# GpSimd scales the softmax weights of the first six attention tiles, and the first phase is written in a new order

## The chip, the cores and the metric

The kernel runs on one core of one Trainium2 chip. Time is device microseconds (us) of one execution; the kernel before has a median of 427.57 us over 3 runs (426.88 to 429.05). Engines: TensorE (PE; PEld is its weight load), VectorE (DVE), ScalarE (ACT), GpSimd (POOL) and SyncE (SP), which issues the DMAs.

## The reference

Three layers in a row, batch 4, sequence 576. Only the first two lie in the part that changes.

```python
# 1: windowed attention, 8 heads of 64
scores = scale * np.matmul(q, k.transpose(0, 1, 3, 2))
mask = (rel >= 0) & (rel < window)            # window = 128
scores = np.where(mask, scores + bias[None], -1000000000.0)
attn = np.exp(scores - max); attn = attn / (attn.sum(-1) + 1e-09)
x = np.matmul(attn, v)
# 2: gated MLP
h = np.maximum(x @ w_in, 0.0); u, v = halves of h
v_n = (v - mean) / sqrt(var + 1e-6)
v_s = w_spatial @ v_n (over the sequence) + b_spatial
x = (u * v_s) @ w_out
# 3: mixture of 4 attention experts, two of them gated in per token (second phase)
```

## The kernel before

**Two phases.** The first phase (up to about 246 us) does layers 1 and 2 up to the gated product, which goes to DRAM. Then follow a fold of `w_out` with the experts' weights, and the second phase, layer 3. Only the first phase changes.

**Tiles and names.** The first attention runs over 20 tiles of 128 queries (the fifth of each batch has 64), numbered 0 to 19 in the order of the list `tiles`; tile n has two groups of four heads, g = 0 and 1. The work is written out by hand as a list of steps, the string `OPENING` (then `FIRST` and `SECOND`): for each engine the order of its instructions is that of the list, and each engine works through its own queue in that order, waiting where data or a buffer is not there. `step()` (L807) turns a name into instructions:

- `rawN`, `qN`, `kN`, `vN`, `Wk.ld`: loads, on SyncE's queue. `CN.x`: turns the 64-bit words of chunk N of `w_in` into two fp32r parts `win`: abs, high, low on ScalarE; shl, or, mask, mul, rest on VectorE (L439 to L442, L263); sum, add, minus, sec on TensorE.
- `sN.g`: scores, TensorE, into one of two `psS` buffers. `lN.g.cp` (L551, L543) and `lN.g.i` (L285): masking copy and row minimum, VectorE. `eN.g.i` (L286): exponential with row sum, ScalarE. `fN.g.add`, `.rec` (L562, L563): the sum's reciprocal, VectorE. `fN.g.mul` (L566): the weights times it, VectorE.
- Tiles 0 to 5 are turned on TensorE: `tN.g` (L615), `cN.g` copies to SBUF (L617, ScalarE), `gN.g.0` and `.1` mask the two key blocks (L624, L625, GpSimd). Tiles from 6 on are "carried": `mN.g` (L565) scales the weights on GpSimd, and they are turned through DRAM (`T`, `w`, `R`).
- `aN` (L648): weights times values, TensorE. `xhN` and `xlN` (L698, L263): high and low part of x, ScalarE and VectorE. `psT` has one buffer: every `t` and every `a` of tiles 0 to 5 takes it in turn, and the next waits until `c`, or `xh` and `xl`, have read it.
- `Vb.t.n` (L712), `Ub.s.m.n` (L775), `Pb.m.s.n` (L790): three passes each of the products with `w_in` and `w_spatial`, TensorE; `r`, `bn`, `ag`, `n`, `N`, `ur`, `pm` take and normalise their results.
- `W0.ld` also issues `pads()` (L481): two memsets of `vtail` and two fills of `vt` on GpSimd (L483, L485).

What a carried and an uncarried tile differ in stands here:

```python
        if carried(b, j):
            ops["m"] = lambda: nc.gpsimd.tensor_tensor(blocks, blocks, sm.unsqueeze(1).unsqueeze(3).to_broadcast([P, 4, n, 32]), op=ALU.mult)
        ops["f.mul"] = lambda: nc.vector.tensor_tensor(p[:, :n, :], p[:, :n, :], sm.unsqueeze(2).to_broadcast([P, n, P]), op=ALU.mult)
```

Of the kernel before, what the change touches and what calls it, by code (L numbers as in the profile page):

```python
# [23 lines left out]
P = 128  # L24
# [21 lines left out]
    l2.1.0 l2.1.1 f1.0.add C2.mask l2.1.2 l2.1.3 C3.or C2.mul f1.0.rec C3.mask e1.1.0 c0.0 C1.low e1.1.3 e1.1.1 C2.high e1.1.2 a0 C2.sum C2.minus s3.1
    C2.sec C3.sum e2.1.3 e2.1.2 xh0 C4.abs C3.high f1.1.add f1.0.mul xl0 f1.1.rec C3.mul f1.1.mul e2.1.0 e2.1.1 C2.low t1.0 c1.0 C3.minus C3.sec
    C3.low t1.1 V0.0.0 V0.0.1 V0.0.2 C5.abs c1.1 g1.0.0 g1.0.1 g1.1.0 g1.1.1 l2.0.cp f2.1.add l2.0.0 l2.0.1 l2.0.2 l2.0.3 f2.1.rec C5.shl e2.0.3
    e2.0.2 e2.0.1 e2.0.0 f2.1.mul l3.1.cp t2.1 l3.1.0 f2.0.add l3.1.1 f2.0.rec l3.1.2 f2.0.mul l3.1.3 s3.0 r0.0 c2.1 t2.0 c2.0 e3.1.3 e3.1.2 s4.1
    g2.1.0 g2.1.1 g2.0.0 g2.0.1 a1 C5.or l3.0.cp l3.0.0 l4.1.cp l3.0.1 e3.1.1 e3.1.0 l3.0.2 l3.0.3 e3.0.3 xh1 e3.0.0 e3.0.1 l4.1.0 l4.1.1 C4.shl C4.or  # L50
    xl1 e3.0.2 f3.1.add f3.1.rec f3.1.mul C5.mask f3.0.add C5.mul C4.mask C4.mul f3.0.rec C5.high raw6 v3 v4 raw7 W0.ld k5 e4.1.0 e4.1.1 s4.0 q5 q6
    W1.ld W1.hi q7 s5.0 a2 xh2 W0.hi V0.1.0 V0.1.1 V0.1.2 C6.abs C7.abs C4.high xl2 f4.1.add f4.1.rec C5.rest f4.1.mul C6.shl C7.shl f3.0.mul t3.1
    C5.add C5.sec c3.1 V0.2.0 t3.0 V0.2.1 g3.1.0 g3.1.1 l4.0.cp C7.or l4.0.0 l4.0.1 c3.0 v5 v6 k10 v7 v8 C4.rest r0.1 g3.0.0 s5.1 C7.high l5.0.cp
    C7.mask C5.low t4.1 q8 V0.2.2 g3.0.1 c4.1 l5.0.0 e4.0.0 l5.0.1 l5.1.cp e4.0.1 C7.rest C4.add g4.1.0 a3 r0.2 l5.1.0 l5.1.1 e5.0.0 f4.0.add C7.mul
    g4.1.1 e5.0.1 e5.1.0 f4.0.rec C6.or e5.1.1 s6.0 v10 xh3 f4.0.mul s6.1 C6.high f5.0.add xl3 C7.add q9 V0.3.0 f5.0.rec C6.rest f5.0.mul t4.0 C6.mask
    C7.sec c4.0 C4.sec l6.0.0 C7.low C6.mul g4.0.0 t5.0 C4.low V0.3.1 l6.0.1 l6.0.2 O0.ld c5.0 l6.0.3 e6.0.0 g4.0.1 f5.1.add V0.3.2 g5.0.0 e6.0.1
    l6.1.0 f5.1.rec bn0.0 e6.0.2 g5.0.1 e6.0.3 a4 f5.1.mul r0.3 l6.1.1 l6.1.2 e6.1.0 l6.1.3 s7.1 f6.0.add bn0.1 v13 xh4 v14 e6.1.1 f6.0.rec xl4 C6.add
    m6.0 e6.1.2 U0.0.0.0 e6.1.3 bn0.2 U0.0.0.1 f6.1.add T6.0 C6.sec t5.1 C6.low s7.0 f6.1.rec l7.1.cp w6.0 m6.1 c5.1 O0.abs bn0.3 U0.0.3.0 l7.1.0
    g5.1.0 U0.0.1.0 l7.1.1 e7.1.0 l7.1.2 g5.1.1 l7.1.3 e7.1.1 T6.1 q14 s8.0 e7.1.2 O1.ld ag0.0 e7.1.3 ag0.1 ag0.2 w6.1 ag0.3 W0.lo n0.2.ln U0.0.0.2
    n0.2.ex f7.1.add a5 n0.2.r0 W1.lo ur0.0.0 f7.1.rec n0.2.r1 O0.shl W4.ld m7.1 U0.0.1.1 l7.0.cp U0.0.2.0 n0.2.r2 R6.0 U0.0.2.1 l7.0.0 l7.0.1 W2.ld  # L60
    U0.0.3.1 e7.0.0 l7.0.2 l7.0.3 e7.0.1 T7.1 U0.0.3.2 e7.0.2 U0.0.1.2 n0.2.r3 e7.0.3 O0.or R6.1 U0.0.2.2 ur0.0.3 w7.1 f7.0.add ur0.0.1 l8.0.cp s8.1
    xh5 f7.0.rec N0.2.sc ur0.0.2 m7.0 xl5 U0.1.1.0 N0.2.hi U0.1.2.0 l8.0.0 q10 W4.hi l8.0.1 l8.0.2 U0.1.1.1 T7.0 e8.0.0 U0.1.1.2 W2.hi l8.0.3 V0.4.0
    N0.0.sc w7.0 ur0.1.1 N0.1.sc e8.0.1 N0.0.hi U0.1.3.0 W4.lo N0.1.hi U0.1.3.1 l8.1.cp e8.0.2 R7.1 V0.4.1 W2.lo e8.0.3 W3.ld l8.1.0 a6 l8.1.1 W5.ld
    e8.1.0 l8.1.2 l8.1.3 e8.1.1 f8.0.add N0.2.lo U0.1.2.1 xh6 f8.0.rec N0.0.lo e8.1.2 U0.1.2.2 m8.0 e8.1.3 R7.0 xl6 V0.4.2 ur0.1.2 f8.1.add s9.1
    N0.1.lo g7.1.0 r0.4 f8.1.rec T8.0 V1.0.0 W5.hi m8.1 l9.1.cp w8.0 V1.0.1 bn0.4 W3.hi g7.1.1 l9.1.0 V1.0.2 l9.1.1 e9.1.0 l9.1.2 g7.0.0 l9.1.3 e9.1.1
    ag0.4 W5.lo U0.1.3.2 n0.4.ln g7.0.1 r1.0 U0.1.0.0 ur0.1.3 T8.1 U0.1.0.1 n0.4.ex e9.1.2 n0.4.r0 W3.lo e9.1.3 s9.0 w8.1 n0.4.r1 f9.1.add a7 bn1.0
    l9.0.cp n0.4.r2 R8.0 f9.1.rec l9.0.0 xc7 U0.1.0.2 m9.1 l9.0.1 q11 l9.0.2 e9.0.0 l9.0.3 k15 s14.1 xs7 ur0.1.0 v11 e9.0.1 s10.1 n0.4.r3 T9.1 xh7
    e9.0.2 N0.3.sc w9.1 V1.1.0 e9.0.3 N0.4.sc N0.3.hi xl7 V1.1.1 N0.4.hi N0.3.lo g8.0.0 P0.0.1.0 l14.1.cp R8.1 f9.0.add U1.0.0.0 l14.1.0 g8.0.1
    l14.1.1 V1.1.2 f9.0.rec e14.1.0 ag1.0 N0.4.lo m9.0 e14.1.1 U1.0.0.1 r1.1 P0.0.1.1 f14.1.add P0.0.0.0 P0.0.1.2 bn1.1 P0.0.0.1 T9.0 R9.1 P0.0.0.2
    l10.1.0 f14.1.rec w9.0 ag1.1 l10.1.1 e10.1.0 U1.0.0.2 m14.1 l10.1.2 e10.1.1 l10.1.3 pm0.0.0 s14.0 g8.1.0 e10.1.2 T14.1 ur1.0.0 s10.0 pm0.0.1  # L70
    e10.1.3 g8.1.1 q13 O0.mask P0.1.1.0 q12 f10.1.add w14.1 P0.1.0.0 O0.mul P0.1.1.1 f10.1.rec g9.1.0 O0.add U1.0.1.0 P0.1.0.1 m10.1 O2.ld P0.1.0.2
    l14.0.cp O0.hi R9.0 l14.0.0 gs0.0 l14.0.1 P0.1.1.2 e14.0.0 pm0.1.0 g9.1.1 O0.sh e14.0.1 T10.1 U1.0.1.1 O1.abs pm0.1.1 U1.0.1.2 w10.1 f14.0.add
    O0.lo a8 ur1.0.1 l10.0.0 f14.0.rec O1.shl e10.0.0 m14.0 l10.0.1 l10.0.2 s11.1 e10.0.1 l10.0.3 O0.sl O1.or xc8 R14.1 g9.0.0 s11.0 T14.0 v12 e10.0.2
    xs8 e10.0.3 gs0.1 P0.2.0.0 g9.0.1 w14.0 O1.mask xh8 P0.3.0.0 P0.2.0.1 xl8 P0.2.0.2 l11.1.cp R10.1 P0.3.0.1 f10.0.add O1.mul q15 P0.3.1.0 pm0.2.0
    g14.1.0 O3.ld P0.3.0.2 l11.1.0 l11.1.1 e11.1.0 l11.1.2 g14.1.1 l11.1.3 V1.2.0 e11.1.1 f10.0.rec O1.add m10.0 e11.1.2 e11.1.3 pm0.3.0 P0.3.1.1
    O1.hi l11.0.cp V1.2.1 O2.abs O1.sh T10.0 P0.2.1.0 l11.0.0 l11.0.1 w10.0 P0.3.1.2 e11.0.0 l11.0.2 l11.0.3 e11.0.1 f11.1.add O1.lo V1.2.2 e11.0.2
    pm0.3.1 e11.0.3 f11.1.rec O2.shl s13.1 r1.2 O1.sl m11.1 f11.0.add gs0.3 s12.1 bn1.2 a9 f11.0.rec T11.1 m11.0 ag1.2 O2.or xc9 R14.0 P0.2.1.1 R10.0
    n1.2.ln P0.2.1.2 n1.2.ex w11.1 xs9 U1.0.3.0 pm0.2.1 xh9 U1.0.3.1 l13.1.cp U1.0.3.2 xl9 v15 V1.3.0 ur1.0.3 l13.1.0 v16 l13.1.1 e13.1.0 l13.1.2
    l13.1.3 gs0.2 V1.3.1 e13.1.1 T11.0 g14.0.0 e13.1.2 n1.2.r0 e13.1.3 s13.0 w11.0 O2.mask g14.0.1 n1.2.r1 V1.3.2 l12.1.cp n1.2.r2 f13.1.add l12.1.0
    U1.1.1.0 q16 r1.3 l12.1.1 l12.1.2 U1.0.2.0 l12.1.3 e12.1.0 n1.2.r3 bn1.3 U1.1.0.0 e12.1.1 e12.1.2 N1.0.sc U1.1.1.1 e12.1.3 ag1.3 N1.2.sc a10  # L80
    n1.3.ln N1.0.hi N1.1.sc n1.3.ex f13.1.rec N1.2.hi f12.1.add l13.0.cp m13.1 U1.1.0.1 N1.1.hi n1.3.r0 U1.1.1.2 l13.0.0 U1.0.2.1 ur1.1.1 n1.3.r1
    l13.0.1 e13.0.0 l13.0.2 U1.1.0.2 l13.0.3 e13.0.1 n1.3.r2 N1.0.lo U1.0.2.2 ur1.1.0 U1.1.3.0 e13.0.2 n1.3.r3 N1.2.lo ur1.0.2 U1.1.3.1 xh10 N1.3.sc
    U1.1.2.0 e13.0.3 N1.1.lo N1.3.hi U1.1.2.1 xl10 U1.1.3.2 N1.3.lo a14 ur1.1.3 f13.0.add T13.1 s12.0 xc14 R11.1 f13.0.rec R11.0 xs14 s15.1 m13.0
    f12.1.rec w13.1 O2.mul xh14 U1.1.2.2 m12.1 P1.0.0.0 ur1.1.2 T13.0 P1.0.0.1 q19 xl14 P1.0.0.2 w13.0 P1.1.0.0 T12.1 P1.1.0.1 g11.1.0 pm1.0.0
    P1.1.0.2 O2.add g11.0.0 w12.1 P1.0.1.0 O2.hi pm1.1.0 P1.1.1.0 l12.0.cp g11.1.1 O3.abs P1.0.1.1 O2.lo g11.0.1 R13.1 P1.0.1.2 O2.sh l12.0.0 l12.0.1
# [1284 lines left out]
```

## Time and profile before

| | |
|---|---|
| median of 3 runs | 427.57 us (426.88 to 429.05) |
| the profiled execution | 427.63 us, its span 425.5 us |
| TensorE busy | 411.5 us (97%) |
| VectorE busy | 315.3 us (74%) |
| ScalarE busy | 243.9 us (57%) |
| GpSimd busy | 156.2 us (37%) |
| mean granted TensorE clock | 0.997 |

The profile is of one execution; its own time is 427.63 us, of which the span from the first to the last instruction is 425.5. "Busy" is the time in which an engine has an instruction under way, so neighbours that overlap count once. A matmul's end is modelled. In a row, `[1.57 <-PE pt L615]` behind an instruction says that its engine was idle 1.57 us before it and what ended that. Rows of one instruction on VectorE or ScalarE overlap the next by a little; the chain of waits counts from start to start.

### The profile page before, as it was taken

The page shows a single profiled execution, that of the slowest core. Times are in us where ns is not written, and L with a number is a line of the kernel's source. Part 1 is how long each engine was busy: PE and PEld are TensorE (multiplying, and loading weights), DVE is VectorE, ACT ScalarE, POOL GpSimd, SP SyncE. Part 2 cuts the span into 40 slices and gives each one's busy share as a digit, 9 for nine tenths or more (in the row PEclk, how much of TensorE's full clock was granted, in tenths as well). Part 3 has the DMA queues.
Part 4 walks back from the last instruction along what each step waited for, and adds up shares of the span by engine and source line. Part 5 has one row for each costly group of instructions (what it writes and reads, how often), then busy time and mean ns, then how long its engine had stood idle before and what let it go on. Part 6 is the DMA issues. An engine that isn't in the chain of part 4 may idle for free.

```text
span 425.5 us, 12102 instructions
## 1 busy us (share of the span) xinstructions
PE 411.5 (97%) x4399; PEld 368.0 (86%) x4399; DVE 315.3 (74%) x1073; ACT 243.9 (57%) x757; POOL 156.2 (37%) x253
## 2 busy tenths in 40 slices
...
GB/s 266 353 332 261 97 197 228 119 256 278 248 222 107 261 201 148 90 102 101 136 262 178 168 105 2 113 0 67 258 184 270 241 153 244 233 258 222 237 226 103
DMA packets 76943, 80.06 MB, mean 188 GB/s; under 512 B 18002, under 2 KB 52946, under 8 KB 76500
## 3 DMA queue, kind: packets, MB, share of 16 engines
...
## 4 chain that ended last, share of the span: by engine, by line
PE 89%; DVE 5%; DMA 2%; ACT 2%; issue 1%; SPq 0%; ACTq 0%; DVEq 0%
PE pu L775 12%; PE pg L790 12%; PE pq L1040 12%; PE pv L712 11%; PE pvB L1068 6%; PE pxB L1237 6%; PE pout_None L1255 5%; PE psB L1134 4%; PE pw L944 4%; PE px L677 3%; PE px L648 2%; PE pg L793 2%; DMA pTB<-mid 1%; PE ps L529 1%; DVE p L285 1%; PE ps L533 1%
## 5 line engine op out<-in xcount | busy, mean ns | idle before, releaser
L286 ACT ACTIVATE p<-p,st 128x128 f32<-128x128 f32 x144 | 56.5, 396 | 19.6 <-DVE st L285 12.8
L775 PE MATMUL pu<-x,win 128*128 128x288 f32 x384 | 59.5, 298 | 0.0
L790 PE MATMUL pg<-wsp,vn 128*128 128x288 f32 x384 | 59.1, 297 | 0.0
L1040 PE MATMUL pq<-x,W 128*128 128x288 f32 x384 | 56.8, 297 | 0.0
L775 PEld LDWEIGHTS pu<-x,win 128*128 128x128 f32 x384 | 54.0, 188 | 3.1 <-issue 1.0
L712 PE MATMUL pv<-win,x 128*128 128x512 f32 x216 | 56.1, 396 | 0.6 <-ACT x L698 0.6
L790 PEld LDWEIGHTS pg<-wsp,vn 128*128 128x128 f32 x384 | 53.5, 188 | 1.4 <-DVE g L798 0.3
L1040 PEld LDWEIGHTS pq<-x,W 128*128 128x128 f32 x384 | 52.5, 188 | 1.6 <-issue 0.8
L565 POOL TENSOR_TENSOR p<-p,st 128x512 f32<-128x512 f32 (+1 forms) x28 | 30.0, 1073 | 60.8 <-ACT p L286 18.7
L1158 ACT ACTIVATE pB<-pB,stB 128x128 f32<-128x128 f32 (+4 forms) x72 | 41.7, 581 | 13.9 <-DVE stB L1150 7.4
L298 POOL TENSOR_SCALAR pB<-pB,stB 128x384 f32<-128x384 f32 (+4 forms) x64 | 35.9, 582 | 28.8 <-DVE stB L1167 14.3
L712 PEld LDWEIGHTS pv<-win,x 128*128 128x128 f32 x216 | 38.6, 188 | 7.8 <-ACT x L698 0.8
L285 DVE CUSTOM_DVE_ANT_0 p<-ps,relm 128x128 f32<-128x128 f32 x128 | 30.2, 282 | 3.0 <-DMA carry<-p 2.6
L1150 DVE CUSTOM_DVE_ANT_0 pB<-psB,trit 128x128 f32<-128x128 f32 (+3 forms) x64 | 27.9, 485 | 6.0 <-PE psB L1134 5.7
L1184 DVE STREAM_TRANSPOSE pB<-pB 128x1024 f32<-128x1024 f32 (+3 forms) x28 | 26.9, 979 | 1.8 <-POOL pB L298 1.7
L286 ACT ACTIVATION_READ_ACCUMULATOR p<-p,st 128x1 f32 x144 | 27.5, 191 | 0.0
L1068 PE MATMUL pvB<-W,x 128*128 128x260 f32 x192 | 27.1, 284 | 0.0
L1255 PE MATMUL pout_None<-wo,o 128*128 128x512 f32 x102 | 26.6, 402 | 0.4 <-ACT o L1245 0.4
L1237 PE MATMUL pxB<-pTB,vt 128*64 128x128 f32 (+2 forms) x480 | 26.4, 260 | 0.5 <-DMA pTB<-mid 0.5
L1237 PEld LDWEIGHTS pxB<-pTB,vt 128*64 128x64 f32 (+1 forms) x480 | 23.3, 136 | 3.4 <-issue 0.9
L798 DVE TENSOR_TENSOR g<-u,pg 128x288 f32<-128x288 f32 x32 | 14.3, 447 | 15.4 <-PE pg L793 12.8
L1068 PEld LDWEIGHTS pvB<-W,x 128*128 128x128 f32 x192 | 24.7, 188 | 0.8 <-issue 0.7
...
## 6 DMA issues: line engine op xcount, KB each, us to landing
...
```

The lines of the kernel that those rows point to most:

```text
L285: lambda: nc.vector.tensor_tensor_reduce(s_view, ps_view, tab, -0.125, FLT_MAX, ALU.add, ALU.min, nm),
L286: lambda: nc.scalar.activation(s_view, s_view, AF.Exp, bias=nm, scale=-1.0, accum_out=sm),
L298: nc.gpsimd.tensor_scalar(p, p, r, 0.0, op0=ALU.mult, op1=ALU.add)
L565: ops["m"] = lambda: nc.gpsimd.tensor_tensor(blocks, blocks, sm.unsqueeze(1).unsqueeze(3).to_broadcast([P, 4, n, 32]), op=ALU.mult)
L712: nc.tensor.matmul(pv, x[i][:, k, t0 : t0 + P], win[j][:, k, 512:1024], start=(n == 0 and k == 0), stop=(n == 2 and k == 3))
L775: nc.tensor.matmul(pu[:, :HALF], win[i][:, k, m * P : (m + 1) * P], x[j][:, k, c], start=(n == 0 and k == 0), stop=(n == 2 and k == 3))
L790: nc.tensor.matmul(pg[:, :HALF], vn[i][k][:, m * P : (m + 1) * P], wsp[j][:, k, c], start=(n == 0 and k == 0), stop=False)
L1040: nc.tensor.matmul(pq[:, :HALF], W[i][c0 // CUT][:, k, c0 % CUT : c0 % CUT + P], G[j][:, k, c], start=(n == k == 0), stop=(n == 2 and k == 3))
L1068: nc.tensor.matmul(pv[:, :260], rows, W[j][1][:, k, 512 - CUT :], start=(n == k == 0), stop=(n == 2 and k == 3))
L1158: nc.scalar.activation(part(i), part(i), AF.Exp, bias=st[:, i : i + 1], scale=-1.0, accum_out=st[:, 4 + i : 5 + i])
L1237: nc.tensor.matmul(px[64 * o : 64 * o + 64, pr, :qn], vt[:kb, c, (2 * pr + o) * 64 : (2 * pr + o) * 64 + 64], rhs(pr, c, o), start=(c == 0 ...
L1255: nc.tensor.matmul(po[:, : c.stop - c.start], o2[i][:, pr, :], wos[j][:, pr, c], start=(n == pr == 0), stop=(n == 2 and pr == 1))
```

## The change

For tiles 0 to 5 the step `fN.g.mul` (VectorE) is replaced by a step `mN.g` on GpSimd that multiplies the same weights by the same reciprocals, and all of `OPENING`, `FIRST` and `SECOND` is written in another order. Later numbers of lines grow by 2 (`t` is L617, GpSimd's new multiply L567).

```diff
 OPENING = """
-    T1 raw0 q0 k0 raw1 C0.abs q1 k1 s0.1+6 s0.0 k2 raw2 q2 raw3 q3 C0.shl C0.or C0.mask C0.mul C0.high T0 l0.1.0 l0.1.1 l0.1.2 l0.1.3 C0.sum C0.minus
...
+    T1 raw0 q0 k0 raw1 C0.abs q1 k1 s0.1+6 s0.0 k2 raw2 q2 raw3 C0.shl C0.or C0.mask C0.mul C0.high T0 reltail k3 v0 k4 v1 C0.sum l0.1.0 l0.0.0 q3
+    e0.1.0 l0.1.1 l0.1.2 C1.abs raw4 l0.1.3 l0.0.1 k5 l0.0.2 e0.1.1 s1.0 l0.0.3 C1.shl e0.1.2 v2 e0.1.3 C1.or C0.minus v3 e0.0.0 s1.1 v4 f0.1.add
...
@@ -563,6 +563,8 @@
         ops["f.rec"] = lambda: nc.vector.reciprocal(sm, sm)
         if carried(b, j):
             ops["m"] = lambda: nc.gpsimd.tensor_tensor(blocks, blocks, sm.unsqueeze(1).unsqueeze(3).to_broadcast([P, 4, n, 32]), op=ALU.mult)
+        else:
+            ops["m"] = lambda: nc.gpsimd.tensor_tensor(p[:, :n, :], p[:, :n, :], sm.unsqueeze(2).to_broadcast([P, n, P]), op=ALU.mult)
         ops["f.mul"] = lambda: nc.vector.tensor_tensor(p[:, :n, :], p[:, :n, :], sm.unsqueeze(2).to_broadcast([P, n, P]), op=ALU.mult)
```

**VectorE, tile 0's first group.** In these rows the name `p_0_1` is tile 0, group 1, `st` its row sums, `ps_1_0` the scores of tile 1, group 0. Before:

```order
L562 TENSOR_TENSOR st_0_1_233<-st_0_1_233,tiny 128x4
L441 TENSOR_SCALAR f_261<-u_107 128x512
L563 RECIPROCAL st_0_1_233<-st_0_1_233 128x4
L442 SCALAR_TENSOR_TENSOR win_101<-raw_187,f_261 128x512
L551 COPY_PREDICATED ps_1_0_242<-lowt,ps_1_0_242 128x4x128
L566 TENSOR_TENSOR p_0_1_232<-p_0_1_232,st_0_1_233 128x512
L285 ISA p_1_0_288,st_1_0_289<-ps_1_0_242,relm 128x128
```

and now:

```order
L562 TENSOR_TENSOR st_0_1_240<-st_0_1_240,tiny 128x4
L551 COPY_PREDICATED ps_1_0_260<-lowt,ps_1_0_260 128x4x128
L563 RECIPROCAL st_0_1_240<-st_0_1_240 128x4
L441 TENSOR_SCALAR f_250<-u_107 128x512
L285 ISA p_1_0_299,st_1_0_300<-ps_1_0_260,relm 128x128
```

The multiply L566 is gone from VectorE, here and eleven times more.

**GpSimd, from the last of the setup on.** `vtail` and `vt` are the pads. Before:

```order
L344 MEMSET pad 1x1 x2
L624 AFFINE_SELECT pU_1_0_444<-pT_1_0_443 128x512
L625 AFFINE_SELECT pT_1_0_443<-pT_1_0_443 128x512
L624 AFFINE_SELECT pU_1_1_455<-pT_1_1_454 128x512
L625 AFFINE_SELECT pT_1_1_454<-pT_1_1_454 128x512
L624 AFFINE_SELECT pU_2_1_501<-pT_2_1_500 128x512
L625 AFFINE_SELECT pT_2_1_500<-pT_2_1_500 128x512
L624 AFFINE_SELECT pU_2_0_531<-pT_2_0_530 128x512
L625 AFFINE_SELECT pT_2_0_530<-pT_2_0_530 128x512
L483 MEMSET vtail_163 64x512
L483 MEMSET vtail_164 64x512
L485 TENSOR_SCALAR vt_0_118<-pad 33x512
```

and now:

```order
L344 MEMSET pad 1x1 x2
L567 TENSOR_TENSOR p_0_1_239<-p_0_1_239,st_0_1_240 128x512
L567 TENSOR_TENSOR p_0_0_242<-p_0_0_242,st_0_0_243 128x512
L483 MEMSET vtail_163 64x512
L483 MEMSET vtail_164 64x512
L485 TENSOR_SCALAR vt_0_118<-pad 33x512
L485 TENSOR_SCALAR vt_0_120<-pad 33x512
L567 TENSOR_TENSOR p_1_0_299<-p_1_0_299,st_1_0_300 128x512
L626 AFFINE_SELECT pU_1_0_399<-pT_1_0_398 128x512
L627 AFFINE_SELECT pT_1_0_398<-pT_1_0_398 128x512
L567 TENSOR_TENSOR p_1_1_366<-p_1_1_366,st_1_1_367 128x512
L567 TENSOR_TENSOR p_2_0_442<-p_2_0_442,st_2_0_443 128x512
```

The scalings stand among the selects, and the pads have moved from behind the selects of tile 2 to a place between the scalings m0.0 and m1.0.

**TensorE, the transpose of tile 1's group 0.** `psw` belongs to the steps C, `pt` is a transpose, `px` an attention, `pv` a V product. Before:

```order
L385 MATMUL psw_425<-u_109,ident 128x512
L615 MATMUL pt_1_0_442<-ident,p_1_0_288 128x128 x4
L387 MATMUL psw_425<-win_100,minus 128x512
L389 MATMUL psw_425<-win_101,one 128x512
L615 MATMUL pt_1_1_453<-ident,p_1_1_348 128x128 x4
L712 MATMUL pv_0_460<-win_100,x_104 128x512 x4
```

and now:

```order
L385 MATMUL psw_370<-u_108,ident 128x512
L617 MATMUL pt_0_0_378<-ident,p_0_0_242 128x128 x4
L387 MATMUL psw_370<-win_100,minus 128x512
L617 MATMUL pt_1_0_397<-ident,p_1_0_299 128x128 x4
L529 MATMUL ps_2_0_408<-k_185,q_2_221 64x192 x2
L531 MATMUL ps_2_0_408<-k_185,q_2_221 64x64
```

t1.0 has moved from behind the attention a0 to a place ahead of the scores s2.0 and s3.1 and of a0, which follow it.

## Rows read from the trace of the kernel before

**Rows 1.** Busy time by stretch: each engine's us (instructions), PEclk, DMA share, GB/s.
```profile
5.00:10.00 5.00, 3.84 (x46) 2.41 (x45) 3.86 (x19) 2.68 (x8) 0.00 (x0) 1.00 1.09 357
10.00:40.00 30.00, 25.22 (x307) 17.96 (x308) 29.65 (x110) 26.65 (x92) 8.63 (x12) 1.00 0.91 312
50.00:75.00 25.00, 25.00 (x291) 21.10 (x293) 24.76 (x100) 19.97 (x72) 9.50 (x13) 1.00 0.71 201
```

**Rows 2.** Waits of TensorE, 0 to 60 us: us in total, times, longest.
```profile
PE pt L615 <- DVE p L566: 1.6, 3, 0.7
PE px L648 <- DVE st L562: 1.6, 1, 1.6
...
PE pt L615 <- ACT f L438: 0.9, 1, 0.9
...
PE pt L615 <- ACT pT L617: 0.4, 1, 0.4
```

**Rows 3.** Waits of TensorE, 60 to 250 us.
```profile
PE pv L712 <- ACT x L698: 0.6, 1, 0.6
```

**Rows 4.** The chain of waits, 0 to 60 us: start us, us, what.
```profile
29.08 0.60 DVE p L566
...
35.61 1.97 PE px L648 x32
...
51.16 1.86 PE pv L712 x8
53.02 1.08 PE px L648 x32
...
57.81 1.25 PE pu L775 x8
...
59.94 0.33 PE pu L775
```

**Rows 5.** Timeline of VectorE: start us, us, what.
```profile
15.36 0.17 DVE L563 RECIPROCAL st<-st 128x4 f32<-128x4 f32 x1
...
26.36 1.11 DVE L566 TENSOR_TENSOR p<-p,st 128x512 f32<-128x512 f32 x1
...
34.79 0.68 DVE L263 TENSOR_TENSOR x<-px,x 128x512 fp32r<-128x512 f32 x1
```

**Rows 6.** VectorE's multiplies by form, 0 to 60 us: busy us, mean ns.
```profile
L566 DVE TENSOR_TENSOR p<-p,st 128x512 f32<-128x512 f32 x8 | 5.9, 738 | 0.0
L566 DVE TENSOR_TENSOR p<-p,st 128x256 f32<-128x256 f32 x4 | 1.6, 412 | 0.0
```

**Rows 7.** Timeline of GpSimd.
```profile
28.99 1.19 POOL L624 TENSOR_SCALAR_AFFINE_SELECT pU<-pT 128x512 f32<-128x512 f32 x1 [2.06 <-ACT pT L617]
...
31.18 0.63 POOL L624 TENSOR_SCALAR_AFFINE_SELECT pU<-pT 128x512 f32<-128x512 f32 x1
...
32.58 0.99 POOL L483 MEMSET vtail<- 64x512 f32 x2
33.65 1.70 POOL L485 TENSOR_SCALAR vt<-pad 33x512 fp32r<-33x512 f32 x2
...
54.90 1.04 POOL L565 TENSOR_TENSOR p<-p,st 128x512 f32<-128x512 f32 x1 [1.91 <-ACT x L698]
```

**Rows 8.** Timeline of TensorE: V0.0 and the start of a1.
```profile
24.39 3.01 PE L712 MATMUL pv<-win,x 128*128 128x512 f32 x12
...
31.23 0.44 PE L648 MATMUL px<-pU,v 128*64 128x128 f32 x4 [0.28 <-POOL pT L625]
```

**Rows 9.** Timeline of ScalarE: two exponentials, a copy.
```profile
15.28 0.40 ACT L286 ACTIVATE p<-p,st 128x128 f32<-128x128 f32 x1
...
16.06 0.39 ACT L286 ACTIVATE p<-p,st 128x128 f32<-128x128 f32 x1
...
30.50 0.59 ACT L617 COPY pT<-pt 128x512 f32<-128x512 f32 x1 [1.57 <-PE pt L615]
```

**Rows 10.** DMA issues, 0 to 60 us: KB each, median us to landing.
```profile
k<-in_kP SPq DMA_DIRECT2D x2, 1152.0 KB, 7.4
```

More of the change, by code (lines that the diff above doesn't have):

```diff
@@ L46 @@
[L46 to L85, printed above, removed]
@@ new lines @@
+    l1.0.cp e0.0.1 v5 C1.high f0.1.rec C0.sec C1.mask C1.sum m0.1 q4 e0.0.2 l1.0.0 l1.0.1 v6 e0.0.3 l1.0.2 l1.0.3 C2.abs W4.ld C1.minus C1.mul t0.1
+    e1.0.0 f0.0.add C2.shl e1.0.1 s2.1 f0.0.rec raw5 e1.0.2 C2.or m0.0 W0.ld e1.0.3 l1.1.cp c0.1 C2.sum f1.0.add C2.high l1.1.0 C3.abs f1.0.rec t0.0
+    l1.1.1 m1.0 l1.1.2 C2.minus C0.low l1.1.3 l2.1.cp c0.0 C3.shl e1.1.0 l2.1.0 t1.0 e1.1.1 l2.1.1 l2.1.2 e1.1.2 s2.0 l2.1.3 C3.or c1.0 s3.1 e1.1.3
+    C2.mask q5 g1.0.0 l2.0.cp C3.high a0 e2.1.0 f1.1.add C3.mask g1.0.1 e2.1.1 l2.0.0 l2.0.1 e2.0.0 l2.0.2 C3.sum l2.0.3 xh0 f1.1.rec C2.mul m1.1
@@ new lines @@
+    e2.0.1 C1.sec xl0 e2.0.2 s3.0 raw7 e2.0.3 C3.mul C1.low C3.minus q6 t1.1 e2.1.2 f2.0.add raw6 f2.0.rec e2.1.3 C2.sec l3.1.cp m2.0 C3.sec c1.1
+    V0.0.0 f2.1.add C2.low l3.1.0 g1.1.0 C3.low f2.1.rec t2.0 l3.1.1 l3.1.2 C4.abs m2.1 l3.1.3 c2.0 s4.0 C4.shl e3.1.0 g1.1.1 e3.1.1 t2.1 C4.or e3.1.2
+    V0.0.1 g2.0.0 c2.1 l3.0.cp e3.1.3 a1 C4.high l4.0.cp g2.1.0 l3.0.0 l3.0.1 C5.abs l3.0.2 g2.0.1 l3.0.3 e3.0.0 f3.1.add e3.0.1 l4.0.0 g2.1.1
+    f3.1.rec l4.0.1 V0.0.2 xh1 v7 C4.rest m3.1 e3.0.2 xl1 e3.0.3 s4.1 r0.0 C4.mask s5.0 e4.0.0 q7 f3.0.add C5.shl e4.0.1 k10 C4.mul W4.hi t3.1 C4.add
```

93 lines of the change are left out of this document (62 added, 31 removed).

## Prediction

> **What bounds the kernel now.** First the windows of busy time [rows 1]: from 10 to 40 us VectorE is busy 29.65 us of 30 and TensorE 25.22, from 50 to 75 us TensorE all 25. The change adds no matmul and removes none. So the question is narrow: how late does TensorE reach the point from which it hardly waits again?
>
> The waits by engine name that loss. In the opening TensorE waits 1.6 us for weights that VectorE has scaled (three transposes t), 1.6 us in one piece under the name of st L562, 0.9 us before t0.1 and 0.4 us for a copy of ScalarE [rows 2], 4.5 us in all; behind 60 us one wait of 0.6 us is left in the phase [rows 3]. The piece of 1.6 us stands in front of a2, the attention of tile 2, where the chain of waits turns to TensorE at 35.61 us [rows 4]. What it waits for is really xl1, the low part of tile 1, which frees the only psT buffer and ran on VectorE from 34.79 to 35.47 [rows 5], with six multiplies f.mul ahead of it in that queue. From a2 on the chain is TensorE without a break, a4 starting at 53.02 [rows 4]. All there is to win is about 4.5 + 0.6 = 5.1 us, 1.2% of the time.
>
> **The change part by part.** *Removed from VectorE.* Twelve multiplies: 8 x 0.738 + 4 x 0.412 = 7.55 us [rows 6]. The next instruction starts before one ends, so the chain counts 0.60 for it [rows 4], half on 256 columns: 8 x 0.60 + 4 x 0.34 = 6.2 us of queue. Ahead of xl4 the new list of VectorE is the old one less these twelve and one reciprocal, nothing else. But VectorE cannot run ahead of what ScalarE and TensorE hand it.
>
> *Added to GpSimd.* Eight scalings of 512 columns and four of 256. The form took 1.04 us at 54.90 [rows 7]: 8 x 1.04 + 4 x 0.52 (half, an estimate) = 10.4 us, and each t gets its weights some 0.4 us later than from VectorE. The Trainium skill (GPSIMD Engine Reference, Engine selection) advises against it: two-input elementwise work belongs on VectorE, GpSimd being about 2x slower. The rows show 1.04 to a mean of 0.738, 1.4x; by 2x a scaling would be 0.4 us longer than its row, and with three on the path below the time would come to 427.6.
>
> *Moved on GpSimd: the pads.* Two memsets of vtail and two fills of vt come with step W0.ld. They took from 32.58 to 35.35, 2.8 us [rows 7], behind the selects of tiles 1 and 2, where little waited. Now they stand between m0.0 and m1.0. f0.0.rec ran at 15.36 [rows 5] and loses f0.1.mul, one mask copy of like length and one row minimum ahead of it, 1.4 us in all: about 14.1. So m0.0 ends near 15.3, the pads near 18.1, m1.0 near 19.1. TensorE has t1.0 in front of s2.0, s3.1 and a0; done with t0.0 and C2.minus by about 16.4, it waits some 2.8 us, a new wait. Its bounds: 1 us, if each of the four takes no more than a select's 0.63 and m0.0 comes early; 3.5 us, if m1.0 is stretched as the select of 1.19 us was [rows 7]. I take 2.8, since the rows are of the pads themselves. With score groups of 0.88 us (59.06 to 59.94 between the two pu pieces [rows 4]) a0 starts near 21.9, its V0.0.0 near 25.4 against 24.39 [rows 8]; VectorE, waiting for s2.0, is idle 1.9 us of what it gained.
>
> *Tiles 2 and 1.* Behind a0 GpSimd has m2.0, g1.1.0, m2.1 and g1.1.1 in a row, 3.5 us at 1.04 and 0.7. t2.1 waits about 1.1 us, and a1 starts near 30.1 against 31.23 [rows 8], with V0.0.2 and s4.1 now behind it and s4.0 ahead.
>
> *ScalarE takes over.* It waited on the transposes before, 1.57 us at 30.50 alone [rows 9], because f.mul was late. In the new list it has, from e1.1.3 (20.8) to c3.1, 18 exponentials and 15 copies, casts and magnitudes. Two exponentials take 0.78 us from start to start (15.28 to 16.06), a copy is busy 0.59 us with some 0.1 of it beside the next [rows 9]: 18 x 0.39 + 15 x 0.5 = 14.5 us. So c3.1 starts no sooner than 35.3, by my walk at 35.8. t3.1 and c3.1 now use the psT buffer ahead of a2: a2 starts near 36.4, 0.8 us later than before, but with t3.1, C4.add, V0.1.0 and C4.sec, 1.8 us of TensorE, already done. Its wait of 1.6 us becomes one of 1.0. With a3 behind small waits for xh2 and xl3, a4 comes near 50.0 (53.02).
>
> *Sum.* Ahead of a4 the new order has the same matmuls, less V0.3.1 and V0.3.2, which took 1.86 us [rows 4] and now come behind it (C7.sec and C6.add cancel). 50.0 + 1.86 = 51.86 against 53.02: 1.2 us earlier. From there TensorE is the limit, and VectorE, busy 24.76 of 25 us between 50 and 75 [rows 1], has 6 us less to do up to the same point, so what hides there today stays hidden. The later 0.6 us I leave standing. The profiled execution took 427.63, 0.06 above the median: 427.63 - 1.2 = **426.4 us**.
>
> *Transfers.* SyncE's list now has k5 (1152 KB, 7.4 us to land [rows 10]) right behind raw4, ahead of q4, v6 and raw5. At the 357 GB/s of 5 to 10 us [rows 1] it costs 3.3 us to all that is queued behind. q4 is wanted near 27 us and raw5 near 31; the 8.0 and 9.4 MB up to them are through by about 25 and 29 at that rate: hidden. If q4 were late by as much as k5 costs, s4.0 would hold t2.1 and a1 for some 1.5 us. Behind them raw7, q6 and raw6 wait in the queue for the end of C3.mul near 25, and are wanted past 36.
>
> *The other 190 us of the phase.* V, U and P keep their number. At its end eleven U groups of 0.53 us stand between V3.2.2 and P3.2.0.0 to cover the last normalisation, some 5 us: nothing, or up to 1 us if the cover is short.
>
> **The rivals.** *Better.* The pads delay little, and the waits at t1.0 and t2.1 shrink from 3.9 to 1.8 us: 426.4 - 2.1 = 424.3, and 423.7 if the later 0.6 us goes too. For it: VectorE is the one engine without idle time from 10 to 40 us, and 6.2 us leave its queue. Against it: the order of GpSimd's queue, and ScalarE's 14.5 us.
>
> *Slower: GpSimd's queue sets the pace.* Working in SBUF together, the two engines slow each other: a select took 1.19 us at 28.99 and 0.63 at 31.18 [rows 7], a multiply of VectorE 1.11 us at 26.36 [rows 5] against a mean of 0.738. Nine GpSimd instructions from m2.0 to m3.1 now stand in a row ahead of t3.1, with no slack by my walk. If six are stretched by 0.55 us, t3.1 and all behind it come 3.3 us later: 429.7. It decides once m2.1 ends past 29 us. The Trainium skill (Perfetto Trace Analysis, Optimizing Scalar/DVE Operations) warns that the two share a port into SBUF, so that moving work between them might not help. The collisions above agree with that warning. Against it: the scaling at 54.90 took 1.04 us with VectorE busy, and the multiplies that collided are gone.
>
> *Nothing that shows.* The waits only change names: 427.6. Or a stall of 1 us comes up later in the new order: 427.4.
>
> **How the numbers follow.** Forecast 0.42, its own range 425.5 to 427.5; better 0.34; GpSimd's queue 0.14; nothing, or a late stall, 0.10. A difference within 0.5% (2.1 us) is about what a measurement of this kernel cannot tell from none. Faster than 425.4 are the better case and a little of the forecast's edge: 0.36. Slower than 429.7 are the upper half of GpSimd's case and, with a late q4 on top or the pads' upper bound, most of the rest of it: 0.14. Within: 0.50. The range runs from 422.9 (all but 0.4 us of the 5.1 us gone) to 429.2.
>
> **What would show it.** Right: no f.mul on VectorE; a wait of TensorE for p from GpSimd of 2 to 3 us between 16 and 19; a0 near 22; ScalarE almost without a gap from 21 to 36; a4 near 50. Better: that first wait under 1 us and a4 under 48.5. Slower: scalings above 1.4 us, a1 after 32, a4 after 52. Wrong altogether: an idle stretch of TensorE over 1 us behind 60 us, or s4.0 waiting for q.

## The result, and the profile after

The change is slower: 431.96 us median of 21 runs (429.61 to 434.04) against 428.37 of 21 runs of the kernel before (424.88 to 432.31); the ratio is 1.0086, 95% interval 1.0063 to 1.0109, some 3.7 us. The profiled execution took 429.61 us, its span 427.9. TensorE's mean granted clock was 0.999 or 1.000 in five of the 21 runs, with a median of 430.4 us, and 0.984 to 0.996 in the others, with 432.1; the profiled one is among the five.

Busy time by stretch in the profile after, to be laid beside [rows 1] (the columns are the same):

```profile
10.00:40.00 30.00, 25.39 (x311) 18.19 (x312) 27.71 (x107) 27.77 (x98) 19.02 (x22) 1.00 1.02 341
50.00:75.00 25.00, 24.94 (x323) 21.85 (x322) 24.05 (x98) 19.54 (x74) 11.77 (x16) 1.00 0.70 198
```

VectorE fell from 29.65 to 27.71 us of 30 (first row), GpSimd rose from 8.63 to 19.02, and TensorE stayed where it was, 25.39 for 25.22. The DMA engines are now full (1.02 for 0.91).

TensorE's waits, 0 to 60 us, answer to [rows 2]:

```profile
PE pt L617 <- POOL p L567: 2.7, 1, 2.7
...
PE ps L527 <- DMA k<-in_kP: 1.4, 1, 1.4
PE ps L525 <- DMA q<-in_qP: 1.1, 1, 1.1
PE px L650 <- ACT pT L619: 0.8, 1, 0.8
```

and 60 to 250 us to [rows 3], where there were 0.6 us in all:

```profile
PE pg L792 <- ACT vn L749: 2.0, 1, 2.0
PE pu L777 <- ACT u L780: 1.7, 2, 1.2
```

The first block says that the opening's old waits for VectorE are gone but for 0.2 us, and new ones, for GpSimd and for q, stand in their place. (The wait for k is at the start of the kernel; it was 0.8 us before, and t0.1 behind it starts at 13.58 us for 13.53.) a4 starts here:

```profile
51.28 0.34 PE L650 MATMUL px<-pU,v 128*64 128x64 f32 x4
```

With the 1.86 us of V0.3 that now come behind it that is 53.14, where it was 53.02 [rows 4]. So in this execution the opening gained nothing and lost next to nothing. (The same opening ran in runs 4 and 5 below; there a4 started at 51.99 and 52.05, with the granted clock lower for some 6 us: see the last section.) The second block is where the time went. The fold's matmuls, the first and last start in each row, before and after:

```profile
L944 PE MATMUL pw<-wc,wt x96: 331/338/344, 246.1 to 262.8; 128*128 128x384 f32 x48, 128*128 128x388 f32 x48
```

```profile
L946 PE MATMUL pw<-wc,wt x96: 333/338/344, 250.6 to 267.3; 128*128 128x384 f32 x48, 128*128 128x388 f32 x48
```

They start 4.5 us later, of which the waits of the second block are 3.7. (In this one pair of profiles the second phase gave back 2.1 us, since the clock of the old one was 0.97 in its last 46 us and it had 0.9 us of waits there.)

The chain of waits from 210 to 231 us shows what made u and vn late:

```profile
212.50 0.44 SPq L902
212.98 3.89 DMA st_wc<-in_wcat
216.89 0.24 ACT wc L266
217.13 7.52 DMA st_wc<-in_wcat
224.67 0.83 ACT wc L266
225.50 0.31 ACT u L780
...
228.44 0.56 DVE vr L745
229.02 0.94 ACT vn L749 x2
...
231.03 0.80 PE pg L792 x4
```

`wcat` holds the projections of the experts, needed by the fold only from 250 us on. Its four pieces are loaded (st_wc, L902) and split into a high part on ScalarE (L266) and a low part on VectorE. These steps, and the eight loads `wt` of the split w_out, stand behind the handwritten `OPENING`; a scheduler puts them among the steps of `FIRST`. SyncE's queue before:

```profile
202.86 0.43 SPq L914 DMA_DIRECT2D trit<-in_tri  x1
...
203.81 0.91 SPq L900 DMA_DIRECT2D st_wc<-in_wcat  x2
214.79 0.33 SPq L875 DMA_DIRECT2D g_dram<-g  x1
215.23 0.87 SPq L900 DMA_DIRECT2D st_wc<-in_wcat  x2
216.15 4.15 SPq L955 DMA_DIRECT2D wt<-wt_dram  x8
```

and after:

```profile
211.65 0.33 SPq L916 DMA_DIRECT2D trit<-in_tri  x1
...
212.50 0.91 SPq L902 DMA_DIRECT2D st_wc<-in_wcat  x2
213.46 2.98 SPq L957 DMA_DIRECT2D wt<-wt_dram  x6
216.56 0.47 SPq L877 DMA_DIRECT2D g_dram<-g  x1
217.13 1.40 SPq L902 DMA_DIRECT2D st_wc<-in_wcat  x2
```

Six `wt` loads have slipped ahead of the second pair of st_wc (in the program's numbering pieces 0 and 1). The first of that pair then lands at 224.67, and ScalarE, which works in order, stands in front of its cast for 4.17 us; before, the same casts waited for nothing and ran at 218.99 and 220.78. ScalarE before and after:

```profile
218.99 0.83 ACT L266 CAST wc<-st_wc 128x772 fp32r<-128x772 f32 x1
```

```profile
224.67 0.83 ACT L266 CAST wc<-st_wc 128x772 fp32r<-128x772 f32 x1 [4.17 <-DMA st_wc<-in_wcat]
225.41 0.40 ACT L780 ACTIVATE u<-pu 128x288 f32<-128x288 f32 x1
```

Behind the cast stand u, which frees one of TensorE's three psD buffers, and the square root of the last normalisation; VectorE waits with it (4.09 us at 225.54, for the low part), with the normalisation N3 behind.

### The profile page after: what moved, and what is told of

Same layout as the page of the kernel before. It is cut to its first block, busy times and chain, and to the rows that moved or that the text cites. A ratio compares the mean times of both kernels' runs of the same rounds, so it can differ in the third digit from the quotient of the medians.

```text
span 427.9 us, 12099 instructions
## 1 busy us (share of the span) xinstructions
PE 410.8 (96%) x4399; PEld 367.5 (86%) x4399; DVE 316.0 (74%) x1061; ACT 242.7 (57%) x757; POOL 171.2 (40%) x265
## 4 chain that ended last, share of the span: by engine, by line
PE 73%; DMA 8%; ACT 7%; DVE 6%; POOL 2%; issue 2%; SPq 2%; DVEq 0%; ACTq 0%; POOLq 0%
PE pq L1042 12%; PE pg L792 10%; PE pv L714 7%; PE pu L777 7%; PE pvB L1070 6%; PE pxB L1239 6%; PE pout_None L1257 6%; PE psB L1136 4%; PE pw L946 4%; ACT p L286 3%; DMA st_wc<-in_wcat 3%; DMA raw<-in_w_in 3%; DMA carry<-p 3%; PE px L679 3%; PE pg L795 2%
## 5 line engine op out<-in xcount | busy, mean ns | idle before, releaser
L777 PE MATMUL pu<-x,win 128*128 128x288 f32 x384 | 58.6, 298 | 2.0 <-ACT u L780 1.7
L714 PE MATMUL pv<-win,x 128*128 128x512 f32 x216 | 57.3, 398 | 0.3 <-ACT x L700 0.3
L565 POOL TENSOR_TENSOR p<-p,st 128x512 f32<-128x512 f32 (+1 forms) x28 | 32.4, 1161 | 61.5 <-DVE st L563 29.2
L285 DVE CUSTOM_DVE_ANT_0 p<-ps,relm 128x128 f32<-128x128 f32 x128 | 30.1, 281 | 3.0 <-DMA carry<-p 2.8
L602 POOL TENSOR_SCALAR_AFFINE_SELECT pU<-pT 128x512 f32<-128x512 f32 (+1 forms) x26 | 18.7, 727 | 21.1 <-DMA pT<-carry 21.0
```

The costliest lines, as they stand in the source:

```text
L285: lambda: nc.vector.tensor_tensor_reduce(s_view, ps_view, tab, -0.125, FLT_MAX, ALU.add, ALU.min, nm),
L714: nc.tensor.matmul(pv, x[i][:, k, t0 : t0 + P], win[j][:, k, 512:1024], start=(n == 0 and k == 0), stop=(n == 2 and k == 3))
L777: nc.tensor.matmul(pu[:, :HALF], win[i][:, k, m * P : (m + 1) * P], x[j][:, k, c], start=(n == 0 and k == 0), stop=(n == 2 and k == 3))
```

## The experiments

Twelve kernels ran, each timed against the kernel before (12 executions, but 6 of order_alone and of pads). Two theories stood at the start: A, the new order loses the time at the end of the phase; B, GpSimd's scalings lose it.

**1. The engine alone (swap_alone).** The old order, `fN.g.mul` replaced in place by `mN.g`, twelve times:

```diff
-    ... f0.1.mul ... f0.0.mul ...
+    ... m0.1 ... m0.0 ...
```

> The old order, with the twelve scalings of tiles 0 to 5 on GpSimd in the places where VectorE had them. Theory A (the loss of the change is made by the new order at the end of the first phase, not by the engine): the end of the phase stays as before, no wait of TensorE over 1 us behind 60 us; in the opening VectorE has 7.6 us less to do and each transpose gets its weights some 0.5 us later, which together lies between 1 us gained and 1 us lost: a ratio of 0.997 to 1.003. Theory B (GpSimd's scalings, stretched by collisions with VectorE, are the loss): slower by 3 us or more, a ratio of 1.007 or over, with waits of TensorE for GpSimd's scalings of some 4 us in all in the opening.

Measured: 426.01 us, ratio 0.9995 (0.9955 to 1.0035), waits of TensorE for scalings 1.1 us in all, behind 60 us one of 1.1 us for a row minimum and none behind 200 us. Theory B falls. But theory A's opening is instructive. VectorE's busy time, third pair of the row, from 0 to 60 us before, with the swap, and without any scaling (run 2):

```profile
0.00:60.00 60.00, 52.64 (x606) 39.55 (x607) 54.80 (x216) 48.62 (x164) 21.61 (x46) 1.00 0.76 250
```

```profile
0.00:60.00 60.00, 55.34 (x611) 41.05 (x611) 54.04 (x207) 49.07 (x165) 33.14 (x58) 1.00 0.78 252
```

```profile
0.00:60.00 60.00, 55.47 (x642) 42.31 (x642) 49.30 (x211) 49.02 (x166) 19.52 (x46) 1.00 0.79 256
```

Multiplies of 7.55 us left VectorE and only 0.8 us of busy time went with them.

**2. No scaling at all (no_scaling).** The old order without `f.mul`; the weights of tiles 0 to 5 stay unscaled.

```diff
-    ... f0.1.mul ... f0.0.mul ...
+    ...
```

> The kernel before, in its old order, with the multiplication of the weights of tiles 0 to 5 by their reciprocals left out altogether, on either engine: the bound of what taking it off VectorE can give. Theory A (GpSimd's scalings take back much of what they save VectorE, in longer instructions of VectorE: with the engine swapped in the old order L562 means 393 ns for 190, L441 541 for 447, L440 871 for 802): without any scaling VectorE's instructions have their durations of before, its busy time between 0 and 60 us falls by 5 us or more (0.8 with the swap), and the time is 1.5 to 3.5 us less than with the swap: a ratio to the kernel before of 0.991 to 0.996. Rival (ScalarE, TensorE and the transfers bound the opening as soon as VectorE is a little freer): as the swap alone, 0.997 to 1.001.

Measured: 425.91 us, 0.9962 (0.9934 to 0.9991). All that can be won in the old order by taking the multiplies off VectorE is thus about 0.4%, 1.6 us; that lies between the two ranges, nearer to A's. What it gains over the swap alone, 1.4 us by the ratios and 0.1 by the medians, can't be told from nothing, since the intervals overlap. VectorE's busy time does fall by 5.5 us. What the swap gives back is, by form (mean ns before the last bar), first with the swap:

```profile
L440 DVE SCALAR_TENSOR_TENSOR u<-raw,u 128x512 int32<-128x512 int32 x8 | 7.0, 871 | 0.1
...
L551 DVE COPY_PREDICATED ps<-lowt,ps 128x512 f32<-128x512 uint16 x7 | 4.8, 683 | 0.4 <-PE ps L533 0.4
L562 DVE TENSOR_TENSOR st<-st,tiny 128x4 f32<-128x4 f32 x11 | 4.3, 393 | 0.3 <-ACT p L286 0.3
```

then without scalings:

```profile
L440 DVE SCALAR_TENSOR_TENSOR u<-raw,u 128x512 int32<-128x512 int32 x8 | 5.5, 685 | 0.1
...
L551 DVE COPY_PREDICATED ps<-lowt,ps 128x512 f32<-128x512 uint16 x8 | 5.5, 686 | 0.4 <-PE ps L533 0.4
L562 DVE TENSOR_TENSOR st<-st,tiny 128x4 f32<-128x4 f32 x11 | 1.7, 154 | 0.3 <-ACT p L286 0.3
```

An addition of four numbers takes 393 ns in the mean with GpSimd's scalings, for 154 without, 2.6 us over eleven of them. What reads the score buffer in PSUM (L551) is not touched. The single instructions of the swap show how. One scaling on GpSimd and one addition on VectorE:

```profile
20.61 1.06 POOL L567 TENSOR_TENSOR p<-p,st 128x512 f32<-128x512 f32 x1 [4.17 <-DVE st L563]
```

```profile
20.70 0.99 DVE L562 TENSOR_TENSOR st<-st,tiny 128x4 f32<-128x4 f32 x1
```

The addition ends at 21.69 us, with the scaling (21.67); two more, at 27.09 and 34.67, also end with a scaling, after 0.85 and 1.00 us, and those that meet none take 0.15 to 0.16. The Trainium skill (SBUF — State Buffer, SBUF: two separate sides) says that VectorE, for an instruction with two inputs in SBUF, and GpSimd take the pair of SBUF ports that they share for a whole instruction, and that the one that comes second blocks. These rows agree: L562 and L440, with both inputs in SBUF, grow, and L551, on PSUM, keeps its 683 ns.

**3. The order alone (order_alone).** The new order with `mN.g`, N under 6, replaced in place by `fN.g.mul`.

```diff
-    ... m0.1 ... m0.0 ... m1.0 ...
+    ... f0.1.mul ... f0.0.mul ... f1.0.mul ...
```

> The new order, with the twelve scalings back on VectorE, in the places where the change has them. Theory A: the waits of TensorE for u and vn between 224 and 231 us, 3.7 us in all, are there as in the change; the wait of 2.7 us at t1.0 is gone, since the pads stand in front of no scaling: 1 to 2 us better than the change in the opening, a ratio to the kernel before of 1.003 to 1.008. Theory B: without GpSimd's scalings the loss is gone: 1.002 or less, also if the waits at the end stay.

Measured: 433.56 us, 1.0141 (1.0084 to 1.0199). The 3.6 us of waits for u and vn are there, and the opening is no better for the pads being out of the way: a4 starts at 53.03, with 1.1 us of wait for VectorE's scaling and 2.4 us for row minima. So the order carries the loss, and in this order GpSimd's scalings are not seen to add to it (the intervals of this run and of the change overlap). That it would beat the change was wrong.

**4. All of wcat ahead of w_out (tail).** The change, with SyncE's order of these loads fixed.

```diff
-    for k in range(2):
-        take_wcat(k)
...
-    later = deque([load_wcat(k) for k in range(4)])
+    with tc.manual_schedule(engines={E_.SP}):
+        for k in (2, 3):
+            take_wcat(k, fp)
+        for k in (0, 1):
+            take_wcat(k)
+        later = deque([load_wcat(k) for k in range(4)])
```

(the loop of the `wt` loads follows inside the block)

> The change, with only the loads of the fold's weights in another order on SyncE: all four pieces of wcat ahead of the eight pieces of w_out (in the change the second pair of wcat stands behind six of these). Theory A (ScalarE, held by a cast that waits 4.2 us for the second pair, is what makes TensorE wait 3.7 us for u and vn): the second pair is issued near 215 us and lands by 219, the casts no longer hold ScalarE over 1 us, and the 3.7 us of waits shrink to under 1 us: 3 to 3.7 us faster than the change, a ratio to the kernel before of 0.998 to 1.002. Rival (the last normalisation is late by itself, since a18 and N3 now stand later in the order; the cast merely waits in the same gap): the waits stay at 2 us or more, 1.004 or over.

Measured: 427.28 us, 0.9997 (0.9967 to 1.0028): 0.9% better than the change by that one order of loads. The casts of the second pair ran at 220.47 and 222.69, the last after 1.07 us of ScalarE's waiting for it (under 1 us was expected), and of the 3.7 us one wait was left:

```profile
PE pu L777 <- ACT vr L723: 0.6, 1, 0.6
```

**5. The same load as late, another engine (cast_pool).** The loads as in the change, the second pair cast and split on GpSimd.

```diff
-        return lambda: split(wc[0][k], wc[1][k], raw_[k])
+        def parts():
+            if k < 2:
+                nc.gpsimd.tensor_scalar(wc[0][k], raw_[k], 1.0, 0.0, op0=ALU.mult, op1=ALU.add)
+                lo_part(wc[1][k], raw_[k], wc[0][k], nc.gpsimd)
+            else:
+                split(wc[0][k], wc[1][k], raw_[k])
+        return parts
```

> The change, with the loads as they are, but the second pair of wcat (the one that lands at 224.7) is cast and split on GpSimd, which is idle there, instead of ScalarE and VectorE. Theory A (it isn't the late load that costs, but that two engines' queues stand behind it: on ScalarE u and the root of the last normalisation, on VectorE that normalisation itself): the load lands as late, near 224, and TensorE's waits for u and vn fall from 3.7 us to under 1 us: a ratio to the kernel before of 0.998 to 1.003, as with the loads reordered. Rival (the end of the phase is slow because of the transfers themselves): the waits stay, 1.006 or over.

Measured: 426.49 us, 0.9985 (0.9963 to 1.0008). GpSimd's timeline has the load landing as late as ever, now with an engine in front of it that nobody waits for:

```profile
225.56 0.88 POOL L937 TENSOR_SCALAR wc<-st_wc 128x772 fp32r<-128x772 f32 x1 [11.57 <-DMA st_wc<-in_wcat]
```

TensorE's waits from 60 to 250 us in that run:

```profile
PE px L679 <- POOL pT L602: 0.6, 1, 0.6
PE pv L714 <- ACT x L700: 0.3, 1, 0.3
```

Nothing is left of the 3.7 us, and the fold starts at 247.4. This settles the cause: not the late load, which the fold can bear, but the two queues that stood behind its cast.

**6. The pads at the start (pads).**

```diff
-                if num[0] == 0:
-                    pads()
...
+    pads()
     for name in OPENING.split():
```

> The change, with the pads (two memsets of vtail, two fills of vt) at the start of GpSimd's queue, where it is idle from 4.4 to 12.2 us. Theory A (the pads are 2.7 us of wait at t1.0, of which ScalarE's queue and late transfers leave part): the wait at t1.0 falls under 0.5 us, a0 starts near 19 instead of 21.6, and a4 0.5 to 2 us earlier than 51.3: a ratio to the kernel before of 1.004 to 1.007. Rival (the loads of q4 and of w_in's sixth chunk set the pace from 27 us on): s4.0 waits longer for q4, a2 stays near 37.5 and a4 near 51.3: 1.008.

Measured: 431.58 us, 1.0113 (1.0065 to 1.0162), so the rival. The wait at t1.0 is gone, a0 starts at 20.22, and then:

```profile
PE ps L525 <- DMA q<-in_qP: 2.7, 1, 2.7
```

The 2.7 us came back whole: s4.0 waits for q4 until 28.84. a4 started at 52.48, 1.2 us later than in the change's profile and 0.4 later than in run 5; TensorE's clock was 0.82, 0.50 and 0.83 in the 2 us stretches from 28 to 34 us, behind this wait, which is 1.7 us at full speed.

**7. k5 behind v6 (k5).**

```diff
-    k5 l0.0.2 e0.1.1 s1.0
+    l0.0.2 e0.1.1 s1.0
...
-    C2.abs W4.ld C1.minus
+    C2.abs k5 W4.ld C1.minus
```

> The change, with the load k5 moved on SyncE from behind raw4 to behind v6, so that v2 to v6, q4 and the room that W4.ld waits for don't stand behind its 1152 KB. Theory A (k5 makes q4 and raw5 late and so takes back what the opening would have won): s4.0 no longer waits for q4 (1.1 us in the change, 2.7 us with the pads at the start), raw5 is issued before 23 instead of at 25.3, a2 starts 0.5 to 1.5 us earlier than 37.5, a4 before 50.5; the waits at the end of the phase stay: a ratio to the kernel before of 1.004 to 1.008. Rival (k5 isn't what is in the way: the transfers as a whole, at some 350 GB/s, are): another load is late instead, s5.0 waiting for k5 itself, a4 at 51 or later: 1.008 or over.

Measured: 431.9 us, 1.0093 (1.0062 to 1.0124). s4.0 no longer waits for q4, and raw5 is issued at 23.45 instead of 25.32; but a2 starts at 38.73 and a4 at 52.54, 1.3 us later than in the change's profile and 0.5 later than in run 5. In this profile the first scores had waited 3.5 us for k, and the clock was 0.91 from 20 to 40 us, so it says little about k5 by itself: inconclusive.

**8 to 11. Together.** `all` is the change with edits 4, 6 and 7; `all_q4` also has q4 ahead of v2; `all_raw5` is `all` with raw5 ahead of W4.ld; `swap_pads` is the swap in the old order with the pads at the start.

The edit of `all_q4`:

```diff
-    e0.1.2 v2 e0.1.3 ... C1.sum m0.1 q4 e0.0.2
+    e0.1.2 q4 v2 e0.1.3 ... C1.sum m0.1 e0.0.2
```

and that of `all_raw5`:

```diff
-    k5 W4.ld C1.minus ... raw5 e1.0.2
+    k5 C1.minus ... raw5 W4.ld e1.0.2
```

> The change with all three: the pads at the start, k5 behind v6, and all of wcat ahead of w_out. Theory A: no wait for GpSimd at t1.0, none for q4, none over 1 us at the end of the phase; a4 at 48.5 to 50.5: 1 to 3 us faster than with the order of wcat alone (a ratio of 0.9997): 0.992 to 0.998. Rival (each wait that goes is followed by the next one, so that a4 stays near 51.5): 0.999 to 1.002.

> As the run with all three, with q4 also moved ahead of v2 to v5. Theory A (q4 is the one late load left): the same or up to 0.5 us faster than all three, 0.991 to 0.998. Rival (v2 to v5 or the loads behind them are then late): 0.5 to 1 us slower than all three, with a wait of TensorE for v.

> As the run with all three, with raw5 also moved ahead of W4.ld. Theory A (with the pads and k5 out of the way ScalarE stands 1.8 us before the magnitude of w_in's sixth chunk, whose load takes 8.8 us because k5 and W4.ld are under way beside it): raw5 lands 1 to 2 us earlier than 31.9, that wait shrinks, a2 starts 0.5 to 1.5 us earlier than 37.5 and a4 before 51: a ratio to the kernel before of 0.994 to 0.998, up to 1 us faster than all three (0.9975). Rival (ScalarE's own work up to c3.1 sets a2): no difference from all three.

> The old order with the scalings of tiles 0 to 5 on GpSimd and the pads at the start of its queue. Theory A (the pads' 2.8 us at 32.6 stand in front of scalings there too, since GpSimd is busy 33 of the first 60 us): TensorE's waits for scalings (1.1 us in the swap alone) fall by half and the time by up to 1 us: a ratio to the kernel before of 0.995 to 0.9995. Rival (nothing waits for GpSimd behind the pads): as the swap alone, 0.998 to 1.001.

Measured: `all` 426.44 us, 0.9975 (0.9944 to 1.0007); `all_q4` 427.41, 0.9978 (0.9947 to 1.0009); `all_raw5` 426.39, 0.9972 (0.9945 to 0.9999); `swap_pads` 425.7, 0.9969 (0.9941 to 0.9997). The four cannot be told from each other. In `all` a1 starts at 29.30, 1.5 us earlier than in the change, and a2 at 37.55, no earlier at all: ScalarE stands in front of the magnitude of w_in's sixth chunk, whose load raw5 takes 8.8 us.

```profile
31.93 0.68 ACT L438 ACTIVATE f<-raw 128x512 f32<-128x512 f32 x1 [1.78 <-DMA raw<-in_w_in]
```

So in the opening the rival of `all` was right for a2 and for a4 (51.35): each wait that goes is followed by the next. Loading raw5 earlier brought a2 to 37.27 and a4 to 51.08, not before 51; with q4 earlier a4 was at 52.70 (clock 0.79 from 32 to 40 us), and no wait for v came of it. In `swap_pads` TensorE's waits for scalings, which were to fall by half, were 1.5 us for 1.1: its ratio is in theory A's range, but not by A's mechanism.

**12. The best of it (best).** The change with the pads at the start, k5 and raw5 as in `all_raw5`, and the cast on GpSimd as in run 5.

```diff
+    pads()
...
+    C2.abs k5 C1.minus ... raw5 W4.ld e1.0.2
...
+                nc.gpsimd.tensor_scalar(wc[0][k], raw_[k], 1.0, 0.0, op0=ALU.mult, op1=ALU.add)
```

> The change with four edits: the pads at the start, k5 behind v6, raw5 ahead of W4.ld, and the second pair of wcat cast and split on GpSimd (its load left where it is). Theory A (the loss at the end and the gain in the opening add up): no wait over 1.6 us anywhere, a4 near 51.1, the fold's first matmul near 246: a ratio to the kernel before of 0.994 to 0.998, faster than the change by 1.1 to 1.5%. Rival (the opening's gain is eaten by the waits that follow): 0.998 to 1.001, as with the cast on GpSimd alone.

Measured: 425.98 us, 0.9961 (0.9932 to 0.9990), a4 at 50.92, the longest wait behind the start 1.1 us, the fold at 247.7 and not near 246. It is faster than the kernel before by 0.4% and than the change by about 1.2% (0.9961 / 1.0086). Its interval overlaps with that of the cast on GpSimd alone (0.9985), so it is not shown that the edits in the opening add anything.

## Why the prediction was wrong

**The step that failed** is "the other 190 us of the phase": "eleven U groups ... stand between V3.2.2 and P3.2.0.0 to cover the last normalisation, some 5 us: nothing, or up to 1 us if the cover is short". It measured 3.7 us. The list has thirteen groups there, not eleven (the old one had sixteen of U and P in that place). They were counted as time on TensorE, and that time was there: from 219.70 TensorE ran nine of them without a wait, and runs 4 and 5 show that thirteen are cover enough. But the normalisation they cover runs on ScalarE and VectorE, and those queues hold, besides the steps written by hand, steps that a scheduler places and that wait for loads on SyncE. The prediction followed SyncE's queue in the opening only. Runs 4 and 5 take the 3.7 us away by two different edits; runs 3, 6 and 7, which leave that place as it is, all keep it.

**"So what hides there today stays hidden"** held from 60 to 200 us (0.5 us of waits, 0.6 before) and failed behind. In the profile after, the memset and the load of trit (a mask of the second phase) wait for a18's matmuls, 4.7 us on GpSimd (trit is given memory that the first attention has left), and all that SyncE has behind it starts at 211.65 instead of 202.86. It comes with the order: in run 1, with the old one, the load of trit is issued at 203.55, in runs 3 to 7 between 212.75 and 215.05. Why this memory came free later, although a18 itself ran no later, at 210.00 for 211.16, was not tried. Of the 4.5 us by which the phase grew, the waits behind 60 us make 3.6 (4.2 in all, for 0.6) and the opening 0.1; the other 0.8 have no wait of their own in the rows, and stay open.

**Transfers: "hidden"** was the second wrong step, of 1.1 us. q4 was issued at 18.76 and landed 9.9 us later, and s4.0 waited for it 1.1 us. The estimate used 357 GB/s throughout; from 20 us on the DMA engines were full and moved less:

```profile
20.00:25.00 5.00, 5.00 (x94) 3.59 (x92) 4.26 (x16) 4.47 (x18) 2.57 (x3) 1.00 1.02 303
25.00:30.00 5.00, 3.91 (x28) 2.87 (x29) 4.66 (x17) 4.82 (x17) 4.04 (x5) 1.00 1.05 259
```

But that is the smaller part. From 0 to 25 us they moved 314 GB/s, so the 8.0 MB up to q4 were through by about 25.6 us, near the 25 forecast; by 28.7, when q4 landed, it was 8.75 MB, and the difference can only be loads issued behind q4. What failed is the assumption that a load has landed as soon as the bytes up to it have moved. In runs 4 and 5, where a0 came 1.5 and 1.7 us later, TensorE waited for no q. The text had named a late q4 as a sign of being wrong altogether, priced it at 1.5 us, and then gave it no more than a corner of one case.

**The opening, step by step.** The wait at t1.0 behind the pads came as reckoned, 2.72 us for 2.8. a0 at 21.64 (21.9), V0.0.0 at 26.08 (25.4), a1 at 30.81 (30.1), a2 at 37.49 (36.4) with a wait of 0.79 (1.0), a4 at 51.28 (50.0). The order of the waits was right but for q4 in t2.1's place; a0 was 0.3 us early, V0.0.0 and a1 0.7 late, a2 1.1 and a4 1.3, and the 1.2 us that the sum had won were gone by a4. Most of it was lost between a0 and V0.0.0, where TensorE never waited (busy 5.00 of 5.00 us from 20 to 25 us): its own work there was taken 0.9 us too short.

**Added to GpSimd.** The scalings' price was too low: eight of 512 columns took 1203 ns in the mean (1.04 us forecast), four of 256 773 ns (0.52). 1.04 us, the one row behind the forecast, is about the least that the larger ones took (1.03 to 1.04, four of the eight); the other four took 1.30 to 1.47.

```profile
L567 POOL TENSOR_TENSOR p<-p,st 128x512 f32<-128x512 f32 x8 | 9.6, 1203 | 13.7 <-DVE st L563 12.4 <-ACT p L286 1.2
...
L567 POOL TENSOR_TENSOR p<-p,st 128x256 f32<-128x256 f32 x4 | 3.1, 773 | 4.9 <-DVE st L563 4.4 <-PE px L650 0.5
```

**Removed from VectorE.** 6.2 us of queue was the gain on paper. Run 1 shows 0.8 us less busy time, and run 2 that even removal without a price is worth about 0.4%. The argument against the collision rival, that the multiplies that collided were gone, was wrong: other instructions of VectorE collide instead.

**The rivals.** GpSimd's queue, at 429.7, came near in number but not in mechanism: its marks, m2.1 past 29, a1 after 32 and a4 after 52, did not show in the profile after (28.6, 30.81, 51.28), and run 3 loses as much with the scalings on VectorE. The two marks of "wrong altogether" both did: a stretch of TensorE's idle time over 1 us behind 60 us, and s4.0 waiting for q.
